# Turning the down product of an FFN's second half: 512 tokens move past 128 output columns, and the residual is turned to match

## The chip, the cores and the metric

The kernel runs on one core of one Trainium2 chip. The metric is device time in microseconds. Three timed runs of the kernel before gave 582.43, 581.5 and 579.44 us: a median of 581.5.

The core's engines each have a queue of instructions that they run in order: TensorE (PE in the profile; its weight loads are PEld), VectorE (DVE), ScalarE (ACT), GpSimd (POOL), and SyncE (SP), which issues all DMAs of this kernel.

## The reference

One block with adaptive layer norm, a long convolution and a gated FFN, on x = q of 2048 tokens by 512 features:

```python
mod = (silu(c) @ w_mod).reshape(1, 6, 1, 512)          # sa, ca, ga, sb, cb, gb
h = layernorm(x) * (1 + ca) + sa
x = x + ga * A(h, k, v, shift_k, ssm_k, ssm_D)         # 4-tap conv of k, times v, a 2048-long conv by FFT, times h
h = layernorm(x) * (1 + cb) + sb
x = x + gb * ((silu(h @ w_gate) * (h @ w_up)) @ w_down)  # 512 -> 1792 -> 512
```

The change touches the last line: the product with `w_down`, and the x to which it is added.

## The kernel before, in words

**Stages.** Up to about 150 us the kernel does the modulation, the convolution (as a transform in matmuls) and the first residual. From then on it is the FFN, and this is where the change lies.

**Blocks and pairs.** The tokens are four blocks of 512 (t = 0 to 3), each kept in a tile `xt[t]` of 128 partitions x 4 x 512: a partition is a token (modulo 128), the last index a feature. The FFN is worked in two pairs: q = 0 with blocks 0 and 1, q = 1 with blocks 2 and 3. The hidden width 1792 is 14 pieces of 128, numbered f. The main loop has one step for each (q, f): n = 2 to 27 (two pieces of the first pair are done earlier, another way), n = 14 * q + f. Below, "step n" is one turn of this loop. `gate_up` computes gate and up of one piece for both blocks of the pair with seven products instead of eight (`seventh`; operands are sums of weight pieces and sums of halves of h). Each of the seven is six matmuls of 128 weights columns against 512 tokens: two halves of the contraction, three passes each, since every float32 is split into two float32r parts, high and low (`PASSES`). Products add into one another in the PSUM banks named `a`, `b`, `c`: before the next product is added to bank `a`, ScalarE copies what is there out to `p1`, `p2`, `r3`. Their order in a step is 1, 7, 6, 2, 5, 3, 4.

**Down.** After two pieces f the down product of this pair of pieces is due. It is fed in between the gate and up products (`feed`, `downs`). For q = 0 it is `down`: for each block and each 128 tokens, the activations are the weights of the matmul (stationary) and 512 columns of `w_down` move past them; VectorE adds the result to `xt` (`x<-x,dn` in the profile). For q = 1, except the last two pieces, it is `down_seven`: again seven products instead of eight, over the 2 x 2 blocks (block of tokens, half of the 512 output features). Each is called twice, for token groups i0 = 0 and 2; a call is two groups of three matmuls whose stationary operand is 128 tokens of an activation and whose moving operand is 256 columns of a combination of `w_down` pieces. Both groups go to one PSUM bank (`da`, `db`, `dc`), and VectorE adds the bank to `xt[2 + t]` (`x<-x,da` and so on). There are six pairs of pieces with `down_seven`; they are worked off in steps 16 to 27, seven calls in each step. The last pair of pieces takes `down` at the end, and its results go to `out`.

**What else is in the first pair's loop.** The kernel normalizes blocks 2 and 3 while the first pair runs, and turns them from token-major to feature-major in three moves: VectorE transposes 32 x 32 squares in place (`half_t`, `n<-n`), SyncE writes the tile to DRAM in runs of 32 floats (`half_put`, four DMAs, `naway<-n`), and reads it back in runs of 128 floats into `raw_h` (`half_get`, eight DMAs, `hraw<-naway`). ScalarE then scales it in place (`half_s`, `hraw<-hraw,modT`). This is done in four halves, (t, h) = (2, 0), (2, 1), (3, 0), (3, 1), put and read back in steps 6, 8, 10 and 11, scaled one step later. Beside it each step loads weights (`ws`), splits them (`split_w`: ScalarE rounds them to `wa`, GpSimd makes four sums `sr`, ScalarE rounds these to `wsum`, GpSimd the low parts), and writes the split weights to DRAM (`store_w`: `dw`, 768 KB, and `ds`, 1 MB) for the second pair, which reads them back (`reload_w`). Every second step loads `wds`, two pieces of `w_down`.

**What sets the order.** Every instruction keeps the order in which the program writes it, on its engine. A call `also(n, k, fn, ...)` puts `fn` behind product k of step n; within a step the keys come in the order 1, 5, 7, 2, 3, 6, 4. The DMAs are one queue of SyncE: a DMA whose data is not ready holds back all behind it. PSUM banks and SBUF slots are dealt out by tables (`SLOTS`).

Of the kernel before, what the change touches and what calls it, by code (L numbers as in the profile page):

```python
# [10 lines left out]
F32 = mybir.dt.float32  # L11
# [5 lines left out]
P = 128  # L17
S = 2048
D = 512
F = 1792  # L20
J = 16
NB = D // P
# [5 lines left out]
G = 2  # L28
# [15 lines left out]
def adaln_h3_swiglu(ctx, tc, q, k0, v0, kT, vT, ssm, dskip, wgu, wdn, wmod, e_fwd, e_inv, w_c, out):  # L44
    nc = tc.nc
    pe, dve, act, pool, sp = (InOrder(tc, e) for e in (nc.tensor, nc.vector, nc.scalar, nc.gpsimd, nc.sync))
# [4 lines left out]
    dp = ctx.enter_context(tc.tile_pool(name="dp", bufs=1, space=bass.MemoryType.DRAM))  # L51
# [61 lines left out]
    def one(name):  # L113
        if "p" not in ffn:
            return bank(name)
        if SLOTS:
            i = int(next(order["one"]))
            return ffn["p"][i // 2].tile([P, 512], F32, tag=f"one{i % 2}", name=name, bufs=1)
        return ffn["p"][0].tile([P, 512], F32, tag="one", name=name)
# [246 lines left out]
    away = {}  # L366
# [186 lines left out]
    xt, st1 = {}, {}  # L553
# [163 lines left out]
    def half_s(t, h):  # L717

        for b in range(NB):
            d = raw_h[0][:, t % 2, b, 2 * h * P : 2 * h * P + 2 * P]  # L720
            act.activation(d, d, AF.Identity, scale=modT[:, 1, b : b + 1], bias=modT[:, 0, b : b + 1])

    BOP, free, slots, held = {}, [], [], {}

    def h_raw(n):
# [35 lines left out]
    stage, AOP, WD, WG = {}, {}, {}, {}  # L761
    NG = NF // G

    def load_w(f):
        st = r4([P, 2, NB, P], F32, "ws")
        sp.dma_start(st, wgu[f])
        stage[f] = st

    def load_wd(g):
        st = r4([P, G, D], F32, "wds")  # L770
        sp.dma_start(st, wdn[g * G * P : (g + 1) * G * P, :].rearrange("(f p) d -> p f d", p=P))
        stage["d", g] = st

    def split_w(f):

        st = stage.pop(f)
        a11, a12, a21, a22 = st[:, 0, 0:2], st[:, 0, 2:4], st[:, 1, 0:2], st[:, 1, 2:4]
        w = ffn["s"].tile([P, 2, 3, 2, P], F32R, tag="wa", name="wa", bufs=2)
        act.copy(w[:, 0, 0:2], st[:, 0].rearrange("p (a k) c -> p a k c", a=2))
        act.copy(w[:, 0, 2], a22)  # L780
        sr = r4([P, 4, 2, P], F32, "sr")
        pool.tensor_tensor(sr[:, 0], a21, a22, op=ALU.add)
        pool.tensor_tensor(sr[:, 1], sr[:, 0], a11, op=ALU.subtract)
        pool.tensor_tensor(sr[:, 2], a11, a21, op=ALU.subtract)
        pool.tensor_tensor(sr[:, 3], a12, sr[:, 1], op=ALU.subtract)
        s = e8([P, 2, 4, 2, P], F32R, "wsum")
        act.copy(s[:, 0], sr)
        pool.tensor_tensor(
            w[:, 1, 0:2], st[:, 0].rearrange("p (a k) c -> p a k c", a=2), w[:, 0, 0:2].bitcast(F32), op=ALU.subtract
        )  # L790
        pool.tensor_tensor(w[:, 1, 2], a22, w[:, 0, 2].bitcast(F32), op=ALU.subtract)
        for i in (0, 2):
            pool.tensor_tensor(s[:, 1, i : i + 2], sr[:, i : i + 2], s[:, 0, i : i + 2].bitcast(F32), op=ALU.subtract)
        set_a(f, w, s)
# [10 lines left out]
    def reload_w(f):  # L805

        w = ffn["s"].tile([P, 2, 3, 2, P], F32R, tag="wa", name="wa", bufs=2)
        s = e8([P, 2, 4, 2, P], F32R, "wsum")
        for d, t in zip(kept[f], (w, s)):
            sp.dma_start(t.bitcast(F32), d)  # L810
        set_a(f, w, s)
# [29 lines left out]
    def split_wd(g):  # L841
        wd_mul(g)
        wd_hi(g)
        wd_lo(g)
# [3 lines left out]
    def wd_sums(g):  # L848

        wd_mul(g)  # L850
        st = stage["d", g]
        h = D // 2
        b11, b12, b21, b22 = st[:, 0, :h], st[:, 0, h:], st[:, 1, :h], st[:, 1, h:]
        tb = r4([P, 4, h], F32, "tb")
        pool.tensor_tensor(tb[:, 0], b12, b11, op=ALU.subtract)
        pool.tensor_tensor(tb[:, 1], b22, tb[:, 0], op=ALU.subtract)
        pool.tensor_tensor(tb[:, 2], b22, b12, op=ALU.subtract)
        pool.tensor_tensor(tb[:, 3], b21, tb[:, 1], op=ALU.subtract)
        stage["t", g] = tb
# [16 lines left out]
    PASSES = ((1, 0), (0, 1), (0, 0))  # L876
# [12 lines left out]
    acts = {}  # L889

    def down(q, g, t, i):

        parts = 2 if (q, g, t, i) == (1, NG - 1, 0, 3) else 1
        for h in range(parts):
            d = slice(h * D // parts, (h + 1) * D // parts)
            o = one("dn")[:, 0 : D // parts]
            for fl in range(G):
                for n, (wa, xa) in enumerate(PASSES):
                    pe.matmul(
                        o, acts[q, g * G + fl, t][:, xa, i * P : (i + 1) * P], WD[g][:, wa, fl, d],  # L900
                        start=(fl == n == 0), stop=(fl == G - 1 and n == 2),
                    )
            xv = xt[2 * q + t][:, i, d]
            dve.tensor_tensor(xv, xv, o, op=ALU.add)
            if g == NG - 1:
                sp.dma_start(out[:, 4 * (2 * q + t) + i, d], xv)
        if i == 3:
            for fl in range(G):
                slots.append(acts.pop((q, g * G + fl, t)))

    todo = []
# [2 lines left out]

    SUM = {1: ("a", 0, 0), 7: ("c", 1, 1), 6: ("a", 1, 0), 2: ("b", 0, 0), 5: ("a", 1, 1), 4: ("c", 1, 0), 3: ("a", 0, 1)}

    def down_seven(g, i0, n, bank_):

        k, t, dh = SUM[n]
        a, b = HOP[g][PROD[n][0]], WT[g][PROD[n][1]]  # L920
        more = k in bank_
        if not more:
            bank_[k] = one("d" + k)
        o = bank_[k].rearrange("p (i d) -> p i d", i=2)
        for ii in range(2):
            for m, (wa, xa) in enumerate(PASSES):
                pe.matmul(
                    o[:, ii], a[:, xa, (i0 + ii) * P : (i0 + ii + 1) * P], b[:, wa],
                    start=(not more and ii == m == 0), stop=(m == 2), skip_group_check=True,
                )  # L930
        xv = xt[2 + t][:, i0 : i0 + 2, dh * (D // 2) : (dh + 1) * (D // 2)]
        dve.tensor_tensor(xv, xv, o, op=ALU.add)
        if i0:
            slots.append(HOP[g].pop(PROD[n][0]))

    def sevens(g):
        for i0 in (0, 2):
            bank_ = {}
            todo.extend(("7", g, i0, n, bank_) for n in SUM)

    def downs(n):
        for _ in range(min(n, len(todo))):
# [124 lines left out]
    def seven(q, f):  # L1067
        return q == 1 and f // G < NG - 1
# [588 lines left out]
    def also(n, k, fn, *a):  # L1657
        AT2.setdefault((n, k), []).append(lambda: fn(*a))

    for n, (t, h) in zip((6, 8, 10, 11), ((2, 0), (2, 1), (3, 0), (3, 1))):  # L1660
        also(n - 1, 2, half_t, t, h, 0)
        also(n - 1, 6, half_t, t, h, 1)
        also(n, 1, half_put, t, h)
        also(n, 3, half_get, t, h)
        also(n + 1, 5, half_s, t, h)
    for n in range(G, 2 * NF):
        q, f = n // NF, n % NF

        at = {k: AT2.get((n, k), []) + ([AT[n, k]] if (n, k) in AT else []) for k in range(1, 8)}
        if n + 1 < 2 * NF:  # L1670
            nf = (n + 1) % NF
            if n + 1 >= NF + G:
                at[1].append(lambda nf=nf: reload_w(nf))
            else:
                at[7].append(lambda nf=nf: split_w(nf))
            if n + 2 < NF + G:
                at[7].append(lambda nf=(n + 2) % NF: load_w(nf))
        g = f // G
        if q:
            if f % G == 0:  # L1680
                at[3].append(lambda g=g: load_wd(g))
            else:
                if seven(q, f):
                    at[1].append(lambda g=g: wd_sums(g))
                    at[3].append(lambda g=g: wd_seven(g))
                else:
                    at[1].append(lambda g=g: split_wd(g))
        elif g + 1 < NG:
            if f % G:
                at[6 if n == G + 1 else 3].append(lambda g=g + 1: split_wd(g))  # L1690
            else:
                at[3].append(lambda g=g + 1: load_wd(g))
        if q == 0:
            at[2].append(lambda f=f: store_w(f))
        if n == NF + 1:
            acts_ = b16("acts2", (P, 4, 2, 512), F32R)
            slots.extend(acts_[:, k] for k in range(4))
            for o in (last["T1"], last["T4"]):
                slots.extend(o[:, k] for k in range(2))
        (gate_up_first if n in (G, NF) else gate_up)(q, f, at)  # L1700
        if f % G == G - 1:
            if seven(q, f):
                sevens(f // G)
            else:
                todo.extend((q, f // G, t, i) for t in (1, 0) for i in range(4))
# [73 lines left out]
```

## Time and profile before

| | |
|---|---|
| timed runs | 582.43, 581.5, 579.44 us |
| profiled execution | span 577.7 us from the first to the last instruction; its own time is not listed apart from the three above |
| TensorE busy | 571.7 us (99%), its weight loads 462.5 (80%) |
| VectorE, ScalarE, GpSimd busy | 448.3 (78%), 306.4 (53%), 318.0 us (55%) |
| granted TensorE clock | 1.0 throughout |
| DMA | 106.98 MB in 54,435 packets, of which 19,441 are under 512 B |

How to read it: the span and the share of an engine tell which engine is the limit on the whole; the rows of the timelines (start, duration, engine, operation, shape, count, and in brackets the idle time before and what ended it) tell what was late at one place. A DMA row of SyncE's queue is the time that issuing took, not the transfer. L40 is the line of a helper through which nearly every instruction is recorded, so instructions are told apart by the names of their tiles.

### The profile page before, as it was taken

To read this page: it belongs to the slowest core of one execution; us is meant where nothing else is said; L and a number is where in the kernel's file an instruction comes from. 1 tells how busy PE (TensorE), PEld (TensorE's weight loads), DVE (VectorE), ACT (ScalarE), POOL (GpSimd) and SP (SyncE) were. 2 spreads that over 40 slices of the span, in tenths; PEclk is the share of its full clock that TensorE was granted. 3 is DMA by queue.
4 is the path that set the end of the run, shared out by engine and by line. 5 is a ranking of instruction groups with operands and counts; after the bars stand their busy time and mean duration, and the time that the engine had idled before them with its cause. 6 is when DMAs were issued, how large, how long until landed. Compare 5 with 4: busy or idle time off the path is not lost.

```text
span 577.7 us, 10729 instructions
## 1 busy us (share of the span) xinstructions
PE 571.7 (99%) x4262; PEld 462.5 (80%) x4262; DVE 448.3 (78%) x622; ACT 306.4 (53%) x471; POOL 318.0 (55%) x298
## 2 busy tenths in 40 slices
PE   9999999999999999999999999999999999999997
PEld 9985476546888888888887888888888888888886
DVE  4999999998998766666576579858686868686766
ACT  3999989951754544445454566343424343434330
POOL 1349897689737866757475676461606161515210
PEclk9999999999999999999999999999999999999999
DMA  8966998998215454284939970454343434343403
GB/s 315 411 256 261 379 251 227 235 235 205 69 37 200 148 216 165 40 281 145 283 140 257 250 319 1 149 190 171 117 160 124 160 123 161 127 162 127 163 1 145
DMA packets 54435, 106.98 MB, mean 185 GB/s; under 512 B 19441, under 2 KB 36209, under 8 KB 48370
## 3 DMA queue, kind: packets, MB, share of 16 engines
q1 hardware_dynamic: 54386, 106.31, 56.0%
q8 instruction: 33, 0.54, 0.4%
q14 instruction: 16, 0.13, 0.1%
HBM read 71.69 MB, written 34.60 MB: 184 GB/s over the span
## 4 chain that ended last, share of the span: by engine, by line
PE 86%; DVE 5%; DMA 4%; ACT 1%; SPq 1%; issue 1%; POOL 0%; ACTq 0%; POOLq 0%; DVEq 0%
PE a L40 22%; PE dn L40 14%; PE c L40 11%; PE b L40 6%; PE da L40 6%; PE s L40 4%; PE g L40 4%; PE dc L40 3%; PE iv L40 3%; PE pk L40 3%; DMA wm<-in_wmod 2%; PE kvt L40 2%; PE px L40 2%; DMA away<-X 1%; PE kt L40 1%; PE db L40 1%
## 5 line engine op out<-in xcount | busy, mean ns | idle before, releaser
L40 PE MATMUL a<-op,wsum 128*128 128x512 f32 x432 | 110.9, 392 | 0.3 <-ACT r L40 0.2
L40 PEld LDWEIGHTS a<-op,wsum 128*128 128x128 f32 x432 | 78.7, 188 | 15.7 <-ACT r L40 0.7
L40 PE MATMUL dn<-wd,acts 128*128 128x512 f32 x360 | 90.4, 389 | 0.0
L40 PEld LDWEIGHTS dn<-wd,acts 128*128 128x128 f32 x360 | 67.5, 188 | 14.0
L40 ACT COPY p<-a 128x512 f32<-128x512 f32 x50 | 29.3, 587 | 57.2 <-PE a L40 57.2
L40 POOL TENSOR_TENSOR wa<-ws,wa 128x512 fp32r<-128x512 f32 (+1 forms) x28 | 32.9, 1196 | 41.1 <-ACT wa L40 41.1
L40 DVE TENSOR_TENSOR x<-x,dn 128x512 f32<-128x512 f32 (+1 forms) x65 | 43.4, 672 | 12.8 <-PE dn L40 12.5
L40 POOL TENSOR_TENSOR tb<-wds 128x256 f32<-128x256 f32 x12 | 8.9, 740 | 64.1 <-DVE wds L40 64.1
L40 DVE TENSOR_TENSOR b<-r,c 128x512 f32<-128x512 f32 x24 | 16.7, 696 | 32.9 <-ACT sg L40 32.9
L40 ACT COPY r<-a 128x512 f32<-128x512 f32 x24 | 14.1, 586 | 50.7 <-PE a L40 50.7
L40 PE MATMUL c<-op,wa 128*128 128x512 f32 x156 | 40.0, 392 | 0.0
L40 PE MATMUL c<-op,wsum 128*128 128x512 f32 x156 | 39.6, 389 | 0.0
L40 DVE STREAM_TRANSPOSE X<-X 128x1024 f32<-128x1024 f32 x16 | 37.6, 2415 | 0.8 <-ACT X L40 0.8
L40 POOL TENSOR_TENSOR wsum<-sr,wsum 128x512 fp32r<-128x512 f32 x28 | 38.1, 1381 | 0.0
L40 PE MATMUL b<-op,wa 128*128 128x512 f32 x144 | 36.9, 391 | 0.0
L40 POOL TENSOR_TENSOR wd<-wds,wd 128x512 fp32r<-128x512 f32 x14 | 18.3, 1329 | 29.1 <-ACT wd L40 29.1
L40 PEld LDWEIGHTS c<-op,wsum 128*128 128x128 f32 x156 | 29.3, 188 | 6.1
L40 DVE TENSOR_TENSOR x<-x,da 128x512 f32<-128x512 f32 x48 | 32.7, 681 | 1.2 <-PE da L40 1.1
L40 PEld LDWEIGHTS c<-op,wa 128*128 128x128 f32 x156 | 28.5, 188 | 5.7 <-DVE b L40 0.4
L40 PEld LDWEIGHTS b<-op,wa 128*128 128x128 f32 x144 | 26.3, 188 | 4.9
L40 POOL TENSOR_TENSOR s<-s,bcs 128x512 f32<-128x512 f32 x22 | 28.0, 1287 | 0.9
L40 POOL TENSOR_TENSOR sr<-ws 128x256 f32<-128x256 f32 x28 | 24.8, 885 | 5.3 <-issue 4.4
(193 smaller groups left out, 1351.1 us busy)
## 6 DMA issues: line engine op xcount, KB each, us to landing
ds<-wsum SPq DMA_DIRECT2D x12, 1024.0 KB, 8.0
wsum<-ds SPq DMA_DIRECT2D x12, 1024.0 KB, 6.4
dw<-wa SPq DMA_DIRECT2D x12, 768.0 KB, 6.3
wa<-dw SPq DMA_DIRECT2D x12, 768.0 KB, 4.3
ws<-in_wgu SPq DMA_DIRECT2D x16, 512.0 KB, 5.4
wds<-in_wdn SPq DMA_DIRECT2D x14, 512.0 KB, 7.1
wm<-in_wmod SPq DMA_DIRECT2D x6, 1024.0 KB, 10.1
away<-X SPq DMA_DIRECT2D x3, 2048.0 KB, 11.8
```

The source lines that it names most:

```text
L40: return lambda *a, **k: self.tc.keep_in_program_order(f(*a, **k))
```

## The change

For q = 1 the down products are computed transposed. A combination of `w_down` pieces, 128 output features wide, is now stationary, and 512 tokens of an activation move past it: three matmuls of 512 columns for a call instead of six of 256. A bank then holds 128 features (partitions) by 512 tokens. `down` swaps its operands in the same way for q = 1. So that the residual can be added, `xt[2]` and `xt[3]` are turned to feature-major in steps 9 to 14 of the loop, by the same three moves as the normalized rows: `x_half` (VectorE, eight instructions in all), `x_put` (four DMAs for each half of a block, 16 in all), `x_get` (eight DMAs for each half, 32 in all). The output tensor has a second half that is feature-major, and the host puts it back in order.

```diff
+    def x_half(t, h, k):
+
+        v = xt[t][:, 2 * h + k].rearrange("p (c x) -> p c x", x=32)
+        dve.transpose(v, v)
+
+    def x_put(t, h):
+
+        v = xt[t][:, 2 * h : 2 * h + 2].rearrange("p k (c x) -> p (k c) x", x=32)
+        m = away["x", t, h] = dp.tile([32, 32, 4, 32], F32, tag=f"x{t}{h}", name=f"xaway{t}{h}")
+        for z in range(4):
+            sp.dma_start(m[:, :, z, :], v[32 * z : 32 * z + 32])
+
+    def x_get(t, h):
+
+        m = away["x", t, h].rearrange("d (k b y) z x -> y k d b (z x)", k=2, y=4)
+        for y in range(4):
+            for k in range(2):
+                i = (2 * h + k) * P
+                sp.dma_start(xt[t][32 * y : 32 * y + 32, :, i : i + P], m[y, k])
...
@@ down
-                    pe.matmul(
-                        o, acts[q, g * G + fl, t][:, xa, i * P : (i + 1) * P], WD[g][:, wa, fl, d],
-                        start=(fl == n == 0), stop=(fl == G - 1 and n == 2),
-                    )
+                    w, x = WD[g][:, wa, fl], acts[q, g * G + fl, t][:, xa]
+                    l, r = (w[:, i * P : (i + 1) * P], x[:, d]) if q else (x[:, i * P : (i + 1) * P], w[:, d])
+                    pe.matmul(o, l, r, start=(fl == n == 0), stop=(fl == G - 1 and n == 2))
             xv = xt[2 * q + t][:, i, d]
             dve.tensor_tensor(xv, xv, o, op=ALU.add)
             if g == NG - 1:
-                sp.dma_start(out[:, 4 * (2 * q + t) + i, d], xv)
+                sp.dma_start(out[q, :, 4 * t + i, d], xv)
...
-    def down_seven(g, i0, n, bank_):
+    def down_seven(g, i, n, bank_):
 
         k, t, dh = SUM[n]
         a, b = HOP[g][PROD[n][0]], WT[g][PROD[n][1]]
         more = k in bank_
         if not more:
             bank_[k] = one("d" + k)
-        o = bank_[k].rearrange("p (i d) -> p i d", i=2)
-        for ii in range(2):
-            for m, (wa, xa) in enumerate(PASSES):
-                pe.matmul(
-                    o[:, ii], a[:, xa, (i0 + ii) * P : (i0 + ii + 1) * P], b[:, wa],
-                    start=(not more and ii == m == 0), stop=(m == 2), skip_group_check=True,
-                )
-        xv = xt[2 + t][:, i0 : i0 + 2, dh * (D // 2) : (dh + 1) * (D // 2)]
+        o = bank_[k]
+        for m, (wa, xa) in enumerate(PASSES):
+            pe.matmul(
+                o, b[:, wa, i * P : (i + 1) * P], a[:, xa],
+                start=(not more and m == 0), stop=(m == 2), skip_group_check=True,
+            )
+        xv = xt[2 + t][:, 2 * dh + i]
         dve.tensor_tensor(xv, xv, o, op=ALU.add)
...
+    for n, t in ((9, 2), (12, 3)):
+        for i in range(4):
+            also(n + i // 2, 3 if i % 2 else 1, x_half, t, i // 2, i % 2)
+        for h in range(2):
+            also(n + 1 + h, 5, x_put, t, h)
+            also(n + 2, 3 + h, x_get, t, h)
...
-    args.append(nc.dram_tensor("out_0", (P, J, D), F32, kind="ExternalOutput").ap())
+    args.append(nc.dram_tensor("out_0", (2, P, J // 2, D), F32, kind="ExternalOutput").ap())
```

How the queues change at the three places that matter below. First SyncE's queue of DMAs in steps 10 to 12. Before (`naway`, `hraw`: the normalized rows of block 3 out and back; `ws`: weights in; `dw`, `ds`: split weights out; `wds`: down weights in):

```order
L40 DMA naway_3297<-n_0_3194 1024x1x32 x4
L40 DMA ws<-in_wgu 128x1024
L40 DMA dw_3363<-wa 128x1536
L40 DMA ds_3364<-wsum 128x2048
L40 DMA hraw<-naway_3297 32x4x128 x8
L40 DMA wds<-in_wdn 128x2x512
L40 DMA naway_3433<-n_1_3327 1024x1x32 x4
L40 DMA ws<-in_wgu 128x1024
L40 DMA dw_3499<-wa 128x1536
L40 DMA ds_3500<-wsum 128x2048
L40 DMA hraw<-naway_3433 32x4x128 x8
L40 DMA ws<-in_wgu 128x1024
```

In the change the same stretch, where `xaway` and `x_788` are block 2's residual out and back:

```order
L40 DMA naway_3299<-n_0_3195 1024x1x32 x4
L40 DMA xaway_3314<-x_788 1024x1x32 x4
L40 DMA ws<-in_wgu 128x1024
L40 DMA dw_3371<-wa 128x1536
L40 DMA ds_3372<-wsum 128x2048
L40 DMA hraw<-naway_3299 32x4x128 x8
```

```order
L40 DMA naway_3442<-n_1_3335 1024x1x32 x4
L40 DMA xaway_3460<-x_788 1024x1x32 x4
L40 DMA ws<-in_wgu 128x1024
L40 DMA dw_3513<-wa 128x1536
L40 DMA ds_3514<-wsum 128x2048
L40 DMA hraw<-naway_3442 32x4x128 x8
L40 DMA x_788<-xaway_3314 32x4x128 x8
L40 DMA x_788<-xaway_3460 32x4x128 x8
L40 DMA ws<-in_wgu 128x1024
```

Four puts of the residual stand in front of the weights' traffic in each of two steps, and 16 gets in front of the next weights.

Second, VectorE in steps 9 and 10 (`wds`: down weights scaled; the transpose of `n` is the last move before `naway` goes out). A piece of the difference, where the rows with numbers in other places are the same instructions:

```order
+L40 TENSOR_TENSOR b<-r_3251,c 128x512
+L40 STREAM_TRANSPOSE x_788<-x_788 128x512
+L40 TENSOR_TENSOR wds<-wds,bcs 128x1024
+L40 TENSOR_TENSOR x_718<-x_718,dn 128x512
+L40 TENSOR_TENSOR a<-sg_3276,b 128x512
+L40 TENSOR_TENSOR acts<-a,acts 128x512
+L40 STREAM_TRANSPOSE n_0_3195<-n_0_3195 128x512
+L40 TENSOR_TENSOR c<-p_3193,c 128x512
+L40 TENSOR_TENSOR c<-sg_3253,c 128x512
+L40 STREAM_TRANSPOSE x_788<-x_788 128x512
+L40 TENSOR_TENSOR acts<-c,acts 128x512
```

The two rows with `x_788` are new; one of them stands ahead of the transpose of `n`.

Third, TensorE at the start of step 16, the first with `down_seven`. Before:

```order
L40 MATMUL a<-spare,wa 128x512 x6
L40 MATMUL c<-op,wsum 128x512 x6
L40 MATMUL da<-wdb,acts 128x256 x6
L40 MATMUL a<-op,wsum 128x512 x6
L40 MATMUL dc<-wdt,acts 128x256 x6
L40 MATMUL b<-op,wa 128x512 x6
```

In the change:

```order
L40 MATMUL a<-spare,wa 128x512 x6
L40 MATMUL c<-op,wsum 128x512 x6
L40 MATMUL da<-acts,wdb 128x512 x3
L40 MATMUL a<-op,wsum 128x512 x6
L40 MATMUL dc<-acts,wdt 128x512 x3
L40 MATMUL b<-op,wa 128x512 x6
```

The groups keep their places; a down group is three wide matmuls instead of six narrow ones.

More of the change, by code (lines that the diff above doesn't have):

```diff
@@ L923, in down_seven @@
             bank_[k] = one("d" + k)
-        o = bank_[k].rearrange("p (i d) -> p i d", i=2)
-        for ii in range(2):
-            for m, (wa, xa) in enumerate(PASSES):
-                pe.matmul(
-                    o[:, ii], a[:, xa, (i0 + ii) * P : (i0 + ii + 1) * P], b[:, wa],
-                    start=(not more and ii == m == 0), stop=(m == 2), skip_group_check=True,
-                )
-        xv = xt[2 + t][:, i0 : i0 + 2, dh * (D // 2) : (dh + 1) * (D // 2)]
+        o = bank_[k]
[5 more added lines that the diff above has]
+        xv = xt[2 + t][:, 2 * dh + i]
         dve.tensor_tensor(xv, xv, o, op=ALU.add)
-        if i0:
+        if i:
             slots.append(HOP[g].pop(PROD[n][0]))
     def sevens(g):
-        for i0 in (0, 2):
+        for i in range(2):
             bank_ = {}
-            todo.extend(("7", g, i0, n, bank_) for n in SUM)
+            todo.extend(("7", g, i, n, bank_) for n in SUM)
     def downs(n):
@@ L1777 @@
     r = run_bass_kernel_spmd(nc, [arrays], core_ids=[0])
-    return r.results[0]["out_0"].reshape(2, 64, J, D).transpose(1, 0, 2, 3).reshape(1, S, D)
+    y = r.results[0]["out_0"]
+    y = np.concatenate([y[0], y[1].reshape(P, 2, NB, 4, P).transpose(4, 1, 3, 2, 0).reshape(P, J // 2, D)], 1)
+    return y.reshape(2, 64, J, D).transpose(1, 0, 2, 3).reshape(1, S, D)
```

## The prediction

> **What bounds the kernel now.** I read the page first (busy times), then the timelines of TensorE, ScalarE and the DMA queue, piece by piece.
>
> ```profile
> PE 571.7 (99%) x4262; PEld 462.5 (80%) x4262; DVE 448.3 (78%) x622; ACT 306.4 (53%) x471; POOL 318.0 (55%) x298
> ```
>
> TensorE is busy 99% of the span. What shortens its stream shortens the run; what makes it wait lengthens it, since there is no other slack to pay from. So I need two things: what a matmul costs in either width, and which of its suppliers is already just in time.
>
> In the timeline of TensorE (start, length; a length overlaps the next row, so the cost of a group is the distance between starts) one step of the second pair reads:
>
> ```profile
> 446.09 1.55 PE L40 MATMUL a<-spare,wa 128*128 128x512 f32 x6
> ...
> 448.83 0.88 PE L40 MATMUL da<-wdb,acts 128*128 128x256 f32 x6
> 449.55 1.55 PE L40 MATMUL a<-op,wsum 128*128 128x512 f32 x6
> 450.94 0.88 PE L40 MATMUL dc<-wdt,acts 128*128 128x256 f32 x6
> ...
> 460.75 1.55 PE L40 MATMUL a<-spare,wa 128*128 128x512 f32 x6
> ```
>
> and two starts of steps in the first pair:
>
> ```profile
> 342.22 1.52 PE L40 MATMUL a<-op,wa 128*128 128x512 f32 x6
> ...
> 357.18 1.52 PE L40 MATMUL a<-spare,wa 128*128 128x512 f32 x6
> ```
>
> In the first pair a step is 11 groups of six 512-wide matmuls: (357.18 - 342.22) / 11 = 1.360 us a group, 226.7 ns a matmul. In the second pair a group of six 256-wide ones takes 449.55 - 448.83 = 0.72 (119 ns each), and the 512-wide group behind it 450.94 - 449.55 = 1.39, 0.03 more than 1.36. The whole step, seven groups of each kind, takes 460.75 - 446.09 = 14.66 us.
>
> **The gain: fewer, wider matmuls.** Six 256-wide matmuls become three 512-wide ones, for the same sum of columns. A step then has 42 + 21 = 63 matmuls of 512 columns, 63 x 226.7 ns = 14.28 us: 0.38 less. There are 12 such steps (six pairs of f with the seven products), so 4.6 us. Lower bound: a 512-wide matmul stays as slow as behind a narrow group, 1.39/2 = 0.695 for three instead of 0.715: 84 x 0.02 = 1.7 us. I take 4.6, since nothing narrow is left beside them and 1.36 is what such neighbours take in the first pair.
>
> [...]
>
> The vector add behind each group keeps its shape:
>
> ```profile
> L40 DVE TENSOR_TENSOR x<-x,dn 128x512 f32<-128x512 f32 x63 | 42.6, 680 | 12.5 <-PE dn L40 12.2
> L40 DVE TENSOR_TENSOR x<-x,da 128x512 f32<-128x512 f32 x48 | 32.7, 681 | 1.2 <-PE da L40 1.1
> ...
> L40 DVE STREAM_TRANSPOSE n<-n 128x512 f32<-128x512 f32 x8 | 5.6, 703 | 0.0
> ```
>
> 680 and 681 ns, so two halves of 256 or one row of 512 cost the same, and the number of adds is unchanged. The last output writes move the same rows of 2 KB. Both at nothing. The eight new transposes have a row of their own shape: 8 x 0.70 = 5.6 us on VectorE, in steps 9, 10, 12 and 13.
>
> **The price: DMAs ahead of the normalized rows.** The new 16 puts (128 KB in runs of 128 B) and 32 gets (64 KB) copy the shapes of the existing naway and hraw transfers, and they share their queue. The steps at which they are issued are those at which blocks 2 and 3 are turned.
>
> ```profile
> ds<-wsum SPq DMA_DIRECT2D x12, 1024.0 KB, 8.0
> ...
> ws<-in_wgu SPq DMA_DIRECT2D x16, 512.0 KB, 5.4
> ...
> naway<-n SPq DMA_DIRECT2D x16, 128.0 KB, 3.2
> hraw<-naway SPq DMA_DIRECT2D x32, 64.0 KB, 5.2
> ```
>
> The queue of SyncE in steps 10 and 11 (start, time that the issues took):
>
> ```profile
> 300.77 2.97 SPq L40 DMA_DIRECT2D naway<-n  x4
> ...
> 305.50 0.37 SPq L40 DMA_DIRECT2D ds<-wsum  x1
> 306.31 7.50 SPq L40 DMA_DIRECT2D hraw<-naway  x8
> ```
>
> ```profile
> 313.51 0.30 SPq L40 DMA_DIRECT2D hraw<-naway  x1
> ```
>
> ```profile
> 315.07 3.93 SPq L40 DMA_DIRECT2D naway<-n  x4
> ...
> 321.53 8.10 SPq L40 DMA_DIRECT2D hraw<-naway  x8
> 329.73 0.38 SPq L40 DMA_DIRECT2D ws<-in_wgu  x1
> ```
>
> The eighth get leaves at 313.51. That is ds's issue, 305.50, plus ds's usual 8.0 us to landing: the last get goes when the weights written back ahead of it are down. In the change four xaway puts stand between naway and ws in both steps, so ws, dw, ds and the gets of hraw move back by what the puts take. The transfer rate there:
>
> ```profile
> 302.00:304.00 2.00, 2.00 (x10) 1.67 (x9) 1.31 (x3) 1.08 (x2) 1.05 (x2) 1.00 0.88 132
> ```
>
> (busy of the engines, then clock, DMA share, GB/s.) The DMA engines are near full, and short runs go at 132 GB/s: 512 KB (524,288 bytes) take 4.0 us. Bounds: 2.97, their issue alone, if the transfer hides under other traffic; 5.4, from 300.77 to the landing that ScalarE waited for below. I take 4.0.
>
> Who waits for hraw? ScalarE scales it in place, in order, and its next instruction copies p2 out of the bank into which TensorE wants to add:
>
> ```profile
> 306.33 0.82 ACT L40 ACTIVATE n<-x,rsb 128x512 f32<-128x512 f32 x1 [3.20 <-DMA naway<-n]
> ...
> 316.57 2.08 ACT L40 ACTIVATE hraw<-hraw,modT 128x256 f32<-128x256 f32 x4 [0.20 <-DMA hraw<-naway]
> 318.56 0.57 ACT L40 COPY p<-a 128x512 f32<-128x512 f32 x1
> ...
> 331.94 2.08 ACT L40 ACTIVATE hraw<-hraw,modT 128x256 f32<-128x256 f32 x4
> 333.93 0.56 ACT L40 COPY p<-a 128x512 f32<-128x512 f32 x1
> ```
>
> ```profile
> 309.45 1.66 PE L40 MATMUL a<-op,wsum 128*128 128x512 f32 x6 [0.24 <-ACT r L40]
> ...
> 321.82 1.52 PE L40 MATMUL a<-op,wsum 128*128 128x512 f32 x6
> ...
> 336.78 1.52 PE L40 MATMUL a<-op,wsum 128*128 128x512 f32 x6
> ```
>
> In step 11 ScalarE already waits for the last get until 316.57; p2 is copied at 319.13, and the fifth product needs bank a at 321.82: slack 2.7 us. In step 12 the copy ends at 334.49 and the product starts at 336.78: slack 2.3. The last get had landed by 331.94, where ScalarE started without a wait; I take 331.7.
>
> Step by step:
> - Step 9 and 10. A transpose of x2 stands ahead of the last transpose of n, so this one comes 0.65 later:
>
> ```profile
> 300.00 0.70 DVE L40 STREAM_TRANSPOSE n<-n 128x512 f32<-128x512 f32 x1
> ```
>
> naway leaves right behind it (300.77), and ScalarE's n at 306.33 had waited 3.20 for its landing, which had made TensorE wait at 309.45 (0.24). No slack is left: +0.65.
> - Step 11. hraw lands 0.65 + 4.0 later, p2 is ready at 319.13 + 4.65 = 323.78, wanted at 321.82 + 0.65: +1.3.
> - Step 12. Behind two sets of puts: 331.7 + 0.65 + 8.0 = 340.35, then 2.55 to the end of the copy, 342.9. Wanted at 336.78 + 1.95 = 338.73: +4.2.
>
> Together 6.1 us. By the bounds of a put: 331.7 + 0.65 + 5.94 + 2.55 - 336.78 = 4.1, and with 5.4 it is 8.9.
>
> The 16 gets of x2 follow, ahead of the weights of the next f (329.73 before). At the median time of such an issue,
>
> ```profile
> L40 SPq DMA_DIRECT2D hraw<-naway x32: 303/720/1294, 245.9 to 329.3; - x32
> ```
>
> 0.72 us, from 329.63 + 8.65 = 338.3 they end at 349.8, and the weights land 5.4 later, at 355.2. GpSimd then makes four sums before ScalarE can round them:
>
> ```profile
> 340.53 1.75 POOL L40 TENSOR_TENSOR sr<-ws 128x256 f32<-128x256 f32 x1
> ...
> 343.76 0.74 POOL L40 TENSOR_TENSOR sr<-ws,sr 128x256 f32<-128x256 f32 x1
> ```
>
> ```profile
> 350.18 1.05 ACT L40 CAST wsum<-sr 128x1024 fp32r<-128x1024 f32 x1
> 353.36 0.59 ACT L40 COPY r<-a 128x512 f32<-128x512 f32 x1 [2.13 <-PE a L40]
> ```
>
> That is 4.0 us, so 359.2 against 350.18 + 6.1 = 356.3. ScalarE is idle 2.13 us in front of its next copy, which ends at 353.95, and TensorE's sixth product wants it at 342.22 + 9 x 1.36 = 354.46: 2.6 of slack against 2.9, so 0.3 us is left over. The four transposes in steps 12 and 13 (2.8 us) are hidden in TensorE's own stall of 4.2; without it they could cost up to that.
>
> The gets of x3 run in step 14, behind the first output row. Eight of them, 8 x 0.72 = 5.8 us, then stand ahead of wds, the first down weights of the second pair:
>
> ```profile
> 365.29 0.43 SPq L40 DMA_DIRECT2D wds<-in_wdn  x1
> ```
>
> ```profile
> 373.68:380.50 6.82, 6.82 (x31) 5.64 (x31) 3.80 (x6) 2.19 (x4) 4.18 (x5) 1.00 0.81 304
> ```
>
> (Busy times of TensorE, its loads, VectorE, ScalarE, GpSimd, then clock and DMA.) By the landing of ws, 5.4, wds then comes at 365.29 + 11.2 = 376.5, 2.8 after VectorE wants it, at 373.68, where the row begins. From there to its add on b at 380.50, which ScalarE waits for, VectorE is busy 3.80 of 6.82 us: its 3.0 us of idle time cover the 2.8. I count nothing; without that cover it would be the 2.8.
>
> Sum: -4.6 + 6.1 + 0.3 = +1.8 us. Profiled span 577.7 becomes 579.5. The span is 3.8 below the median of 581.5 that the runs show, and which of them the profile belongs to is not shown; I carry the difference over: 583.3 us.
>
> **Rivals.**
> - *Covered.* The puts' short runs overlap with the write-back and delay hraw by less than 2.3 us in all; only the 0.65 stays. 581.5 - 4.6 + 0.65 = 577.6. For it: no row shows a put behind another put. Against: the whole slack is one put set's issue time, and there are two sets. 0.15.
> - *Slower: the weights behind the 16 gets.* If each get costs the 0.94 us that eight took in the crowded queue (7.50/8), the weights leave at 353.3, land at 358.7, and the sums are done at 362.7, 6.4 late; less 2.6 of slack that is a stall of 3.8 where I count 0.3. 583.3 + 3.5 = 586.8. It decides from a landing of the weights after about 355. Against: those eight had 2.25 MB ahead of them, these have only gets. 0.15.
> - *The change does not do what it says:* wide matmuls keep the slower pace of 0.695 per three, gain 1.7: 586.2. For it: no other pace is seen in the second pair; against, every 512-wide neighbour in the first pair. 0.07. [...]
>
> **How the numbers follow.** My forecast has 0.63, with its own range of 581.0 to 586.1 (puts at 2.97 with nothing behind; at 5.4). About 0.5% (2.9 us) is what a measurement of this kernel can tell from no change: below 578.6 or above 584.4. Faster: the covered rival and 0.03 of mine, 0.18. Slower: the two rivals above 584.4, 0.22, and about 0.12 of mine with dear puts: 0.34. Same: the rest, 0.48. The range leaves out most of the covered rival and a little above: 578.0 to 587.0.
>
> **What would show it.** Second pair: steps of 14.28 us, groups of three at 0.68; 14.5 or more speaks for the narrow gain. Steps 11 and 12: ScalarE idle in front of hraw, released by the DMA, about 4 and 8 us, with TensorE waiting for p2 in front of its fifth product 1.3 and 4.2 us. Step 13: the wait of ScalarE for the sums tells how late the weights were. If TensorE shows no idle time between 309 and 345, the price was wrong and the run is near 577; if idle time stands elsewhere, at the first adds into the turned rows or at the reloads, I missed a wait.

## The result, and the profile after

| | before | after |
|---|---|---|
| median of the timed runs | 581.68 us (579.44 to 582.43) | 585.52 us (583.25 to 586.58) |
| ratio, with its 95% interval | | 1.0068, 1.0047 to 1.0088 |

The changed kernel is slower by 0.68%, 3.8 us. The forecast was 583.3 us.

The head of the profile's page after:

```profile
span 583.7 us, 10271 instructions
PE 571.6 (98%) x4010; PEld 450.3 (77%) x4010; DVE 454.3 (78%) x630; ACT 307.1 (53%) x471; POOL 316.7 (54%) x298
```

252 matmuls fewer, and TensorE is as long busy as before (571.7). The profiled execution took 585.51 us, 1.8 more than its span. So the profile of before, with a span of 577.7, stands for a run of about 579.5, the lowest of its six. Of the 6.0 us between the two spans, 1.7 lie ahead of step 9 (TensorE starts it at 281.56 before and at 283.30 after), where both kernels issue the same instructions; in the ten traces of this study step 9 starts between 281.30 and 284.02. Another 0.4 lie behind step 27. The rest is read from the starts of the steps on TensorE:

| | before | after | forecast of the difference |
|---|---|---|---|
| step 9 | 15.24 | 15.51 | |
| step 10 | 15.50 | 16.32 | +0.65 (with step 9) |
| step 11 | 14.96 | 16.46 | +1.3 |
| step 12 | 14.96 | 19.86 | +4.2 |
| steps 13 to 15 | 3 x 14.96 | 3 x 14.96 | +0.3 |
| steps 16 to 27, up to the end of their products | 176.40 | 172.76 | -4.6 |
| sum | | +3.85 | +1.8 |

The sum of the steps, 3.85 us, agrees with the difference of the medians, 3.84.

SyncE's queue in steps 10 to 12 after (start, time that the issues took):

```profile
303.38 2.97 SPq L40 DMA_DIRECT2D naway<-n  x4
306.39 3.59 SPq L40 DMA_DIRECT2D xaway<-x  x4
...
311.75 0.36 SPq L40 DMA_DIRECT2D ds<-wsum  x1
312.16 9.47 SPq L40 DMA_DIRECT2D hraw<-naway  x8
...
322.22 3.76 SPq L40 DMA_DIRECT2D naway<-n  x4
326.03 3.54 SPq L40 DMA_DIRECT2D xaway<-x  x4
...
331.69 8.20 SPq L40 DMA_DIRECT2D hraw<-naway  x8
339.95 8.23 SPq L40 DMA_DIRECT2D x<-xaway  x16
348.28 0.37 SPq L40 DMA_DIRECT2D ws<-in_wgu  x1
```

The two sets of residual puts stand ahead of the weights and of the gets of hraw, as the order of the instructions said. ScalarE after, in the same stretch:

```profile
309.15 0.82 ACT L40 ACTIVATE n<-x,rsb 128x512 f32<-128x512 f32 x1 [3.40 <-DMA naway<-n]
...
323.42 2.08 ACT L40 ACTIVATE hraw<-hraw,modT 128x256 f32<-128x256 f32 x4 [4.23 <-DMA hraw<-naway]
325.40 0.56 ACT L40 COPY p<-a 128x512 f32<-128x512 f32 x1
...
341.74 2.07 ACT L40 ACTIVATE hraw<-hraw,modT 128x256 f32<-128x256 f32 x4 [5.18 <-DMA x<-xaway]
343.72 0.56 ACT L40 COPY p<-a 128x512 f32<-128x512 f32 x1
```

The waits for hraw were 0.20 and none before; they are 4.23 and 5.18 now. (The second is put down to a get of x; what the instruction reads is hraw, and the gets of both lie in one queue.) Behind each scaling stands the copy of p2, and TensorE waits for it:

```profile
326.01 1.66 PE L40 MATMUL a<-op,wsum 128*128 128x512 f32 x6 [1.20 <-ACT p L40]
...
339.75 1.52 PE L40 MATMUL dn<-wd,acts 128*128 128x512 f32 x6
344.33 2.93 PE L40 MATMUL a<-op,wsum 128*128 128x512 f32 x6 [3.07 <-ACT p L40]
347.06 1.83 PE L40 MATMUL dn<-wd,acts 128*128 128x512 f32 x6
348.73 1.53 PE L40 MATMUL a<-op,wsum 128*128 128x512 f32 x6
350.10 1.52 PE L40 MATMUL c<-op,wa 128*128 128x512 f32 x6
```

Idle 1.20 and 3.07 us. But the six matmuls behind the longer wait took 347.06 - 344.33 = 2.73 us instead of 1.36, and the next six 1.67. That is 1.7 us that no wait accounts for. The granted clock in short windows around it (stretch, length, busy of the engines, then clock, DMA share and GB/s):

```profile
344.10:344.20 0.10, 0.00 (x0) 0.00 (x0) 0.10 (x1) 0.10 (x2) 0.00 (x0) 1.00 0.15 21
344.20:344.30 0.10, 0.00 (x0) 0.00 (x0) 0.10 (x1) 0.10 (x2) 0.00 (x0) 0.75 0.05 5
344.30:344.40 0.10, 0.07 (x1) 0.07 (x1) 0.10 (x1) 0.10 (x1) 0.00 (x0) 0.50 0.07 10
...
347.60:347.70 0.10, 0.10 (x2) 0.10 (x1) 0.00 (x0) 0.10 (x1) 0.10 (x1) 0.69 0.72 205
347.70:347.80 0.10, 0.10 (x1) 0.07 (x1) 0.00 (x0) 0.10 (x1) 0.10 (x1) 1.00 0.31 87
```

At about 344.25, still in the idle time, the clock falls to half, and at 347.66 it is whole again: 3.41 us at half speed cost the 1.7.

In the second pair, one step of the changed kernel (step 18) and the load that is late in it (rows of TensorE's timeline, then one of its weight loads):

```profile
425.43 1.52 PE L40 MATMUL a<-spare,wa 128*128 128x512 f32 x6
...
434.27 0.84 PE L40 MATMUL db<-acts,wdb 128*128 128x512 f32 x3
434.96 0.96 PE L40 MATMUL da<-acts,wdt 128*128 128x512 f32 x3
435.76 1.53 PE L40 MATMUL a<-op,wsum 128*128 128x512 f32 x6
...
439.85 1.52 PE L40 MATMUL a<-spare,wa 128*128 128x512 f32 x6
```

```profile
434.96 0.53 PEld L40 LDWEIGHTS da<-acts,wdt 128*128 128x128 f32 x3 [0.27 <-DVE x L40]
```

An undisturbed group of three takes 0.68 and an undisturbed step 14.28, as forecast. This step takes 14.42: the load for the third product into bank da waits for VectorE's add out of that bank. It is so in every second step, and the first step (16) takes 14.82. In step 16 the kernel before had a delay at the same group already; the row of before, then the one of after:

```profile
397.04 0.98 PE L40 MATMUL da<-wdt,acts 128*128 128x256 f32 x6
...
406.26 0.96 PE L40 MATMUL da<-acts,wdt 128*128 128x512 f32 x3 [0.25 <-DVE x L40]
```

In the trace before this group and the `db` group ahead of it take 0.82 and 0.92 us instead of 0.71, the group's first weight load having waited 0.25 for VectorE's add, and step 16 takes 14.96 where the steps behind it take 14.66 to 14.68.

### The profile page after: what moved, and what is told of

It reads as the page before. It is cut to its first block, busy times and chain, and to the rows that moved or that the text cites. A ratio compares the mean times of both kernels' runs of the same rounds, so it can differ in the third digit from the quotient of the medians.

```text
span 583.7 us, 10271 instructions
## 1 busy us (share of the span) xinstructions
PE 571.6 (98%) x4010; PEld 450.3 (77%) x4010; DVE 454.3 (78%) x630; ACT 307.1 (53%) x471; POOL 316.7 (54%) x298
## 4 chain that ended last, share of the span: by engine, by line
PE 72%; DMA 10%; ACT 7%; DVE 5%; issue 3%; SPq 2%; POOL 1%; ACTq 0%; DVEq 0%; POOLq 0%
PE a L40 18%; PE dn L40 10%; PE c L40 9%; PE da L40 6%; PE b L40 5%; PE g L40 4%; DMA ds<-wsum 3%; PE iv L40 3%; PE dc L40 3%; PE s L40 3%; PE pk L40 2%; DMA wm<-in_wmod 2%; DMA hraw<-naway 2%; PE kvt L40 2%; SPq L40 2%
## 5 line engine op out<-in xcount | busy, mean ns | idle before, releaser
L40 PEld LDWEIGHTS a<-op,wsum 128*128 128x128 f32 x432 | 81.6, 190 | 23.6 <-ACT p L40 5.6
L40 PE MATMUL dn<-wd,acts 128*128 128x512 f32 x336 | 85.3, 390 | 0.1
L40 PEld LDWEIGHTS dn<-wd,acts 128*128 128x128 f32 x336 | 63.4, 189 | 13.8 <-DVE acts L40 0.5
L40 POOL TENSOR_TENSOR sr<-ws 128x256 f32<-128x256 f32 x28 | 22.7, 810 | 10.1 <-DMA ws<-in_wgu 5.7
```

The lines of the kernel that those rows point to most:

```text
L40: return lambda *a, **k: self.tc.keep_in_program_order(f(*a, **k))
```

## The experiments

My theory: the new matmuls bring 4 to 5 us less the wait on VectorE; the turning costs 7 to 8 us, nearly all of it by the two sets of puts ahead of hraw, and 1.7 of it by the clock. Rivals: the turning costs by its transposes or by traffic wherever it stands; the slow matmuls of step 12 are slow by the traffic and not by the idle time.

**1. The down product alone.** The loop that issues the turning is left out.

```diff
-    for n, t in ((9, 2), (12, 3)):
-        for i in range(4):
-            also(n + i // 2, 3 if i % 2 else 1, x_half, t, i // 2, i % 2)
-        for h in range(2):
-            also(n + 1 + h, 5, x_put, t, h)
-            also(n + 2, 3 + h, x_get, t, h)
```

> The transposed down product alone: the residual of blocks 2 and 3 is not turned, so the second pair adds feature-major sums to token-major rows and that half of the output is left wrong. Theory (the gain is in the second pair, the price is paid in the first pair's DMA queue): the steps of the second pair run as in the changed kernel, 14.28 and 14.42 us, and no new idle time stands in steps 9 to 13: 581.7 - 3.6 = 578.1 us, faster by 0.6%. Rival (part of the loss belongs to the wide matmuls themselves): 581 or more.

Measured: 578.02 us against 581.05, ratio 0.9945 (0.9930 to 0.9959); the theory had 578.1. Steps 10 to 15 have the lengths of before (15.50, then 14.96 each); the second pair reads as in the change, 14.28 and 14.42 in turn.

**2. The turning alone.** The kernel before, with `x_half`, `x_put`, `x_get` and the loop above, and the old down product.

> The turning alone: the down product is as before (token-major), while the residual of blocks 2 and 3 is turned, so that half of the output is left wrong. Theory: the whole price of steps 9 to 12 as in the changed kernel, 0.3 + 0.8 + 1.5 + 4.9 = 7.5 us: 589.2 us, 1.3% slower. Rival (the price needs the rest of the change, or is scatter between profiles): 582 to 585 us.

Measured: 589.78 us against 581.05, ratio 1.0159 (1.0130 to 1.0188). The parts, -3.0 and +8.7, make +5.7 where both together measured +3.8. The trace shows part of that: in TensorE's timeline of step 12

```profile
344.87 2.92 PE L40 MATMUL a<-op,wsum 128*128 128x512 f32 x6 [3.27 <-ACT p L40]
347.60 2.76 PE L40 MATMUL dn<-wd,acts 128*128 128x512 f32 x6
350.16 1.79 PE L40 MATMUL a<-op,wsum 128*128 128x512 f32 x6
351.79 1.52 PE L40 MATMUL c<-op,wa 128*128 128x512 f32 x6
```

three groups are slow, not two: 351.79 - 344.87 - 3 x 1.36 = 2.8 us lost, 1.1 more than in the change. But step 11 lost less here, 15.50 against 16.46, so steps 11 and 12 together take 36.73 us against 36.32, only 0.4 more. Another 0.8 stands in step 9, which varies between traces with and without the turning; the rest of the 1.9 stays open. The clock windows:

```profile
343.80:343.90 0.10, 0.00 (x0) 0.00 (x0) 0.10 (x1) 0.10 (x2) 0.00 (x0) 0.80 0.78 220
343.90:344.00 0.10, 0.00 (x0) 0.00 (x0) 0.10 (x1) 0.10 (x1) 0.00 (x0) 0.50 0.89 261
...
350.60:350.70 0.10, 0.10 (x2) 0.10 (x1) 0.10 (x1) 0.00 (x0) 0.00 (x0) 0.56 0.00 0
350.70:350.80 0.10, 0.10 (x2) 0.10 (x1) 0.10 (x1) 0.00 (x0) 0.00 (x0) 1.00 0.00 0
```

Half speed from 343.86 to 350.69, 6.83 us: twice the 3.41 of the change.

**3. The puts behind hraw.** The change with the same transposes, puts and gets; only block 2's puts and gets come later in the queue (block 3's lines are as they were).

```diff
-        for h in range(2):
-            also(n + 1 + h, 5, x_put, t, h)
-            also(n + 2, 3 + h, x_get, t, h)
+    for h in range(2):
+        also(12, 3, x_put, 2, h)
+        also(13, 6, x_get, 2, h)
+        also(13 + h, 5, x_put, 3, h)
+        also(14, 3 + h, x_get, 3, h)
```

> The changed kernel, with the puts of block 2's residual moved behind the normalized rows' gets of step 11 and step 12's weights, its gets to step 13; the transposes stay where they are. Theory (the puts delay the normalized rows only by standing ahead of them in the queue): ScalarE waits under 1 us for them in steps 11 and 12, these steps are back at 14.96 us, and only the transposes' 0.3 and 0.7 us in steps 9 and 10 stay: 579.1 us. Rival (the DMA traffic as such costs, wherever it stands): the same 6 us of stall, now in steps 13 and 14: 585 us.

Measured: 577.78 us against 581.05, ratio 0.9949 (0.9932 to 0.9966), 1.3 better than I had expected. ScalarE:

```profile
318.46 2.08 ACT L40 ACTIVATE hraw<-hraw,modT 128x256 f32<-128x256 f32 x4 [0.47 <-DMA hraw<-naway]
...
333.87 2.08 ACT L40 ACTIVATE hraw<-hraw,modT 128x256 f32<-128x256 f32 x4 [0.19 <-DMA hraw<-naway]
```

and SyncE's queue behind it:

```profile
332.82 16.19 SPq L40 DMA_DIRECT2D xaway<-x  x12
349.11 0.82 SPq L40 DMA_DIRECT2D ws<-in_wgu  x1
```

The waits for hraw are gone, and steps 11 to 15 take 14.96 each. The same bytes in the same runs of 128 B, 16 us of issues ahead of the next weights, cost nothing there. So it is the place of the transfers that costs. Block 2's gets moved with the puts here; experiments 5 and 6 tell the two apart. Step 10 keeps 16.15, where experiment 1, without transposes, has 15.50: the transpose ahead of n is worth 0.65.

**4. The transposes moved as well.** As 3, but the eight transposes stand in steps 11 to 13, behind the transposes of n, and block 3's puts and gets move by a few products within steps 13 and 14.

```diff
-    for n, t in ((9, 2), (12, 3)):
-        for i in range(4):
-            also(n + i // 2, 3 if i % 2 else 1, x_half, t, i // 2, i % 2)
+    for (n, k), (t, h, i) in zip(
+        ((11, 1), (11, 5), (11, 2), (11, 2), (12, 1), (12, 5), (12, 2), (13, 1)),
+        ((t, h, i) for t in (2, 3) for h in range(2) for i in range(2)),
+    ):
+        also(n, k, x_half, t, h, i)
```

> As the kernel with the puts moved behind, and the eight transposes moved to steps 11 to 13, where VectorE has gaps, all gets ahead of the first output rows. Theory: no step of the first pair is longer than 15.0 us except step 10 with its old 0.24: 578.1 us, 0.6% faster than the kernel before. Rival: VectorE, full in step 13, or the weights of step 13 behind eight puts, stall TensorE by 1 to 3 us: 579 to 581 us.

Measured: 578.91 us against 581.05, ratio 0.9969 (0.9950 to 0.9987). Step 10 is down to 15.57, and steps 11 to 13 keep 14.96, but step 16 takes 15.08. Its interval overlaps that of 3: no gain beside it can be told.

**5. One set of puts early.** As 3, with the first set of block 2's puts back in its place ahead of hraw, and the second behind.

```diff
-        also(12, 3, x_put, 2, h)
+    also(10, 5, x_put, 2, 0)
+    also(12, 3, x_put, 2, 1)
```

> The changed kernel with only the first set of block 2's puts (four DMAs) ahead of the normalized rows, in step 10; the second set stands behind step 12's weights. Theory (each set ahead of the gets delays them by what it takes, about 4 us, and the delays add): step 11 is as long as in the changed kernel (16.5 us, stall 1.3 to 1.5), step 12 has no stall (14.96 us), because 3.2 - 4.0 leaves nothing. Rival (step 12's stall comes from the bulk of traffic, not from the second set): step 12 stays over 17 us.

One run, 579.68 us (before: 580.45). ScalarE's waits and TensorE's stall:

```profile
321.97 2.09 ACT L40 ACTIVATE hraw<-hraw,modT 128x256 f32<-128x256 f32 x4 [3.56 <-DMA hraw<-naway]
...
337.13 2.09 ACT L40 ACTIVATE hraw<-hraw,modT 128x256 f32<-128x256 f32 x4 [2.00 <-DMA hraw<-naway]
```

```profile
324.58 1.67 PE L40 MATMUL a<-op,wsum 128*128 128x512 f32 x6 [0.56 <-ACT p L40]
```

Step 11 takes 15.85 (I had expected 16.5), step 12 15.17 instead of 19.86: the large stall goes with the second set. Step 13 gained 0.66, where TensorE waited 0.37 for an add of VectorE on b, which I had not expected.

**6. One and a half sets early.** As 5, with two of the second set's four puts back in step 11, to get a stall that is shorter than 3 us in the same place.

```diff
-    also(12, 3, x_put, 2, 1)
+    also(11, 5, x_put, 2, 1, range(2))
+    also(12, 3, x_put, 2, 1, range(2, 4))
```

> As the kernel with one set early, with two of the second set's four puts ahead of the gets in step 11. In the changed kernel step 12 was 4.90 us too long: a stall of 3.2 and then 1.7 us in which the granted clock was about 0.5. Theory (half a set is 2 us; the lower clock comes only behind a long idle time): the stall is 3.2 - 2.0 = 1.2 us, the granted clock stays 1.0 as it did behind the 1.2 us of step 11, and step 12 lasts 16.2 us. Rival (every idle microsecond costs half another one in clock): 16.8 us and a clock below 1.

One run, 581.93 us. TensorE's row and the clock over the stall and the matmuls behind it:

```profile
342.03 1.66 PE L40 MATMUL a<-op,wsum 128*128 128x512 f32 x6 [1.23 <-ACT p L40]
```

```profile
336.00:342.00 6.00, 4.80 (x22) 3.63 (x20) 4.16 (x7) 2.63 (x7) 1.07 (x2) 1.00 0.88 218
342.00:348.00 6.00, 5.97 (x26) 4.95 (x27) 3.48 (x4) 4.37 (x7) 5.43 (x5) 1.00 1.00 320
```

The stall is 1.23, and the clock stays at 1.00 beside a DMA share of 1.00 (320 GB/s). In the change the slow matmuls ran beside a DMA share of about 0.45. So traffic alone, at a share of 1.00, did not make them slow. The step took 16.50, 0.3 more than I had expected and 0.3 less than the rival had; the stall and the clock are what decides between them, since the six matmuls behind the wait took 343.52 - 342.03 = 1.49 us, at a clock of 1.00, and not the 2.73 of the change.

Counted from the start of step 9, the scaling of hraw in step 12 began at 54.76 us with one set ahead (experiment 5), 56.45 with one and a half (339.43 - 282.98 in 6) and 58.44 with two (the change). The gets stand late in 5 and 6 and early in the change, yet the last half set costs 1.99 where the one before costs 1.69. So the early gets can add little: 0.3 us, if half a set costs the same each time (0.5 when counted from the start of step 11).

**7 and 8. The wait of the second pair removed.** The load that is late waits for an add of VectorE, and in front of that add VectorE had waited for ScalarE, to subtract the low part of one operand of the next down product (`S4`). In 7 (as 4) and 8 (as 3) this subtraction is issued later, behind the feeds of the fourth product:

```diff
-                operand(g, "S4", x)
+                h = HOP.setdefault(g, {})["S4"] = slots.pop(0)
+                act.copy(h[:, 0], x)
+                lows.append((h, x))
...
         behind(4)
+        for h, x in lows:
+            dve.tensor_tensor(h[:, 1], x, h[:, 0].bitcast(F32), op=ALU.subtract)
+        lows.clear()
```

> The kernel with transposes and puts moved, and in the second pair VectorE's low part of operand S4 is computed behind its add of the sixth product instead of ahead of it. In the changed kernel every second step of the second pair is 14.42 instead of 14.28 us, with the load for the fifth product waiting for VectorE's add. Theory (this add is late because of the low part that waits 0.65 us for ScalarE): all twelve steps are 14.28 us, 0.14 x 6 + 0.4 = 1.2 us less than with the puts and transposes moved alone: 577 us. Rival (the add is late for another reason, or the next wait comes right behind): no difference.

> The kernel with only the puts and gets moved, and the same order of VectorE's low part in the second pair. Theory: 1.2 us less than with the puts moved alone: 576.6 us, and 0.5 to 1 us slower or equal to the one with the transposes moved as well, since two transposes still stand ahead of the last transpose of the normalized rows in steps 9 and 10 (0.7 us there).

Measured, against 580.45: 7 took 576.26 us, ratio 0.9926 (0.9909 to 0.9943); 8 took 576.15 us, ratio 0.9926 (0.9909 to 0.9943). VectorE in step 18 of the change, and at the same place in step 20 of 7:

```profile
433.03 0.69 DVE L40 TENSOR_TENSOR acts<-c,acts 128x512 fp32r<-128x512 f32 x1 [0.66 <-ACT acts L40]
433.63 0.69 DVE L40 TENSOR_TENSOR b<-p,b 128x512 f32<-128x512 f32 x1
434.23 0.68 DVE L40 TENSOR_TENSOR x<-x,da 128x512 f32<-128x512 f32 x1
```

```profile
452.45 0.69 DVE L40 TENSOR_TENSOR b<-p,b 128x512 f32<-128x512 f32 x1
453.13 0.69 DVE L40 TENSOR_TENSOR x<-x,da 128x512 f32<-128x512 f32 x1
453.74 0.68 DVE L40 TENSOR_TENSOR op<-c,op 128x512 fp32r<-128x512 f32 x1
```

The subtraction (first row there, last row here; its tile is a slot that goes by the name of its first user) now stands behind the add into x. All eleven steps from 16 to 26 take 14.28 in both kernels: 157.08 us against 161.72 before and 158.32 in the change. Step 27, which the theory had at 14.28 too, takes 14.43 in both: there the group for the second product into da takes 0.80 (553.03 - 552.23 in 7) and not 0.68; in the change the load for this group waits 0.28 for VectorE's add. Both are faster than the kernel before and the change. Between them no difference can be told, although step 10 is 0.54 shorter in 7.

The length of steps 9 to 26 on TensorE gives one number for each trace, which the scatter ahead of step 9 does not touch. (Step 9 itself, 15.24 to 16.09 in the traces, is in it.) Beside it stands the difference of the medians (one run for 5 and 6):

| | steps 9 to 26 | against before | medians |
|---|---|---|---|
| before | 267.26 | | |
| change | 271.35 | +4.09 | +3.84 |
| 1, down alone | 264.28 | -2.98 | -3.03 |
| 2, turning alone | 275.75 | +8.49 | +8.73 |
| 3, puts behind | 265.37 | -1.89 | -3.27 |
| 4, transposes too | 264.72 | -2.54 | -2.14 |
| 5, one set early | 266.92 | -0.34 | -0.77 |
| 6, one and a half | 268.57 | +1.31 | +1.48 |
| 7 | 263.41 | -3.85 | -4.19 |
| 8 | 263.99 | -3.27 | -4.30 |

Except in 3 and 8, the two columns agree within 0.5 us. In those two the timed runs are 1.0 to 1.4 better than the steps. Step 9 can be part of it, 15.24 before and 16.09 and 15.84 here, but in 7, where it is 15.91, the columns agree; why is open, and so is the 1.3 by which 3 beat its expectation.

## Why the prediction was right or wrong

The sign was right, and 585.5 lies in the range of 578.0 to 587.0 and near the upper end of the likeliest case's own, 581.0 to 586.1. No difference that can be told had the largest chance (0.48); what came was slower (0.34), 2.2 us above the forecast. Step by step:

- **Pace of the wide matmuls: right.** 0.68 a group of three and 14.28 a step were forecast, and steps 16 to 26 of 7 and 8 have them. The rival that they keep 0.695 falls: 0.68 us for three is 227 ns a matmul, the 226.7 of the first pair.
- **The gain of 4.6: mis-sized, 3.64 measured.** The step "the number of adds is unchanged, at nothing" failed. The adds cost the same (681 ns), but in a shorter step one of them came too late for the bank's next group: 0.14 us in every second step and more in step 16. Experiments 7 and 8 show it, since with the late subtraction moved steps 16 to 26 take 14.28 each. Steps 16 to 27 then take 157.08 + 14.43 = 171.51 us, 4.89 less than before. That is the 4.6 and the 0.28 by which step 16 was already longer in the kernel before; the twelve steps of 14.66 in the sum passed over this step, where the wait for VectorE's add could be seen.
- **Transpose ahead of n, +0.65: right.** Step 10 gained 0.82, and experiment 1 against 3 gives 0.65. Step 9 varies between 15.24 and 16.09 in the traces, with and without transposes (15.66 in experiment 1, 16.09 in 3), so its 0.27 is not put down to the change.
- **A set of puts takes 4.0: about right.** Counted from the start of step 9, ScalarE began the scaling of step 11 5.1 us later than before (323.42 - 283.30 against 316.57 - 281.56), forecast 4.65; in step 12 at 58.4, forecast 340.35 - 281.56 = 58.8. By experiments 5 and 6 the second set took 1.69 + 1.99 = 3.7.
- **Stall of step 11, +1.3: right,** 1.20 idle and 1.50 in the step's length.
- **Stall of step 12, +4.2: mis-sized, 4.90.** The copy of p2 was as late as forecast. TensorE idled less, 3.07, since the steps ahead were longer than I had counted (by 2.6, not 1.95). I took the price of an idle time to be its length; the clock added 1.7. This term (0.7) and the gain (1.0) are most of the 2.05 us by which the sum was low; steps 9 to 11 add 0.6, and the weights that were not late take 0.3 off.
- **Weights behind the 16 gets, +0.3, and the slower rival: wrong, nothing measured.** A get took 8.23 / 16 = 0.51 us and not 0.72, let alone the rival's 0.94. GpSimd began the sums 69.5 us after step 9, forecast (355.2 - 281.56) 73.6:

```profile
352.81 0.74 POOL L40 TENSOR_TENSOR sr<-ws 128x256 f32<-128x256 f32 x1 [3.45 <-DMA ws<-in_wgu]
```

 Step 13 took 14.97. In experiment 3 the same weights stood behind twelve puts and cost nothing either.
- **Transposes of steps 12 and 13, hidden in the stall:** their cover was not needed. Experiment 3 has them without a stall, in steps of 14.96.
- **Late wds in step 15: right at nothing,** the step took 14.95.
- **The rival "covered": falls for the change,** and is what experiment 3 made of it by another order: 577.78 measured, 577.6 in the rival. That these are so near is luck in part: the steps of 3 are 1.89 shorter than before, where the rival had 3.95.
- **The 3.8 us from span to median:** 1.8 lie outside the span in the run after. The rest, 2.0, puts the profile of before among the fastest runs; it fits the scatter ahead of step 9, 2.7 us in the ten traces, but no second trace of the kernel before shows it. Carrying it over from median to median was right.

## What to carry to other kernels

Here DMAs that nobody waited for had a price by their place in the queue: the turning cost 7.1 us in one place (271.35 - 264.28) and 1.1 in another (265.37 - 264.28), by the table of the steps; 0.4 of the 1.1 is step 9's scatter. So ask which later transfer is already just in time, and put the new ones behind it. When a bound engine's step is shortened, look again at what frees its banks: here the next wait was for VectorE's add, 0.27 us in step 18, and the step took 14.42 us where 14.28 was forecast.

## What was not expected of the hardware

The long idle times of TensorE cost more than their length. Over the stall of 1.20 us in step 11 of the change, over that of 1.23 us in experiment 6, and for the six microseconds behind each, the clock was read at 1.00. With the idle times of 3.07 us (the change) and 3.27 us (experiment 2) the granted clock was 0.50, for 3.41 and 6.83 us, and six matmuls in it took twice as long: 2.73 us in both, where 1.36 is the undisturbed group. The drop came 3.0 us and 2.3 us after the idle time began (344.25 - 341.26 and 343.86 - 341.60). Between 1.23 and 3.07 us these steps have no idle time, so from what length on the clock falls is not shown.

The end of the kernels adds to this. The clock falls to 0.50 behind TensorE's last matmul as well, 3.0 us after it in the change (580.20 to 583.18) and 3.9 us after it before (574.64 to 578.54, behind the end of the span of 577.7). So the four drops came 2.3 to 3.9 us into an idle time, and how late one comes differs from trace to trace. What sets the moment is not shown.
